# Fused attention and gated convolution: sums' guard planned behind the values, planner costs corrected, pair 0's rows on two queues, last product in two bank pairs, new order tables

## The chip, the cores and the metric

One core of one Trainium2 chip runs the whole kernel in one launch. The metric is device time in microseconds (us) of that core; a run's time is that of one execution, and the median over runs is what counts.

## The reference

```python
# attention: B=8, H=8, S=576, D=64
scores = q @ k.T / sqrt(D)
cum = cumsum(max(s, 0))
bias = -(cum[:, None] - cum[None, :])
scores = where(causal, -1e9, scores + minimum(bias, 0))
scores = scores - scores.max(-1)
attn = exp(scores); attn = attn / (attn.sum(-1) + 1e-9)
x = concat_heads(attn @ v)                 # 8 x 576 x 512
# mixture part: d_ff=1024, kernel 3
h = maximum(x @ w_in, 0)
conv = depthwise_conv3(h, conv_w)          # along the sequence
out = (h * sigmoid(conv)) @ w_out
```

All in float32; products are made of split high and low parts (three matmuls for one).

## The kernel before

The 64 heads go in 32 pairs (`pair(p)`), each head on one half of the 128 partitions. For a pair, TensorE (PE) makes shift scores for row maxima (`sh`, L1103), VectorE (DVE) reduces them (`mx`, L1120 and L1140), PE makes the transposed scores (`sc`, L1227), ScalarE (ACT) exponentiates them into the single tile `pt` (`ex`, L1244), and PE forms the row sums (`sum`, L1330) and then the values (`pv`, L1278), back to back, in one pair of PSUM banks (`pvs`). What follows the sums is a chain: ACT's **guard** (`gd`, L1347) copies them out with a small constant added into `rs`; two DMAs fold them (`fo`, L1353); DVE takes the reciprocal (`inv`, L1360); a DMA stores it (`ri`, L1365) and two spread it (`rb`, L1375). The values are copied out by `vn` (L1384, ACT or DVE), multiplied (`nm`, L1387) and split into `x` (`xh` L1404, `xl` L1408). Four pairs make one batch entry. Its mixture part is `moe_h` (product L1443, relu `re` L1464, convolution centre `ce` L1478 or L1480 and taps L1493, gate `ga` L1507, `mu` L1513, split `uh` L1522 and `ul` L1527), and `moe_o` (product L1591, copies out `oe` L1622 and L1624, stores L1634 and L1637).

PSUM is four pairs of banks (`ps0` to `ps3`), taken by `psb()`. `moe_o` keeps its two output tiles in the two banks of one pair, and the two copies out (`oe`) are separate tasks.

Nothing is ordered by the source. Each step is a task with a cost per engine, dependencies and a tag (its due time plus a shift from the table `DUE`). `Sched.play` runs a list scheduler on these costs, and the instructions of each engine are then emitted in the planned starting order, and every engine works its list strictly in that order. Where the plan leaves PE idle for longer than 0.6 on its clock, filler matmuls on `mask` are put in (`stay_awake`, L1655). Bulk loads (over 200 KB) are limited to two in flight (`FLY`): the third waits for the first.

The guard's dependency in the plan of before, and the first of the two loads for pair 0's rows:

```python
t_grd = add(f"gd{p}", [("ACT", c_act(RS))], [t_sum], tq, guard, alloc=[ri], uses=[pvs])
...
t_e0 = add("dr0", on, [t_cum, *t_pads], -163, d_rows, alloc=[ek], nbytes=42000)
```

Of the kernel before, what the change touches and what calls it, by code (L numbers as in the profile page):

```python
# [35 lines left out]
NDR, NDS = 0, 0  # L36
# [59 lines left out]
    "pads":  # L96
        "0 -413.8 1 1.58 2 -45.35",
    "ind":
# [395 lines left out]
def kernel(  # L494
# [145 lines left out]
    def c_act(n, ptr=0):  # L640
        return 0.19 + n / 1.2e3 + 0.09 * ptr
# [1091 lines left out]
```

## Time and profile before

| what | value |
|---|---|
| runs | 810.8, 808.15, 808.61 us; median 808.61 us |
| profiled execution | 812.8 us, of which the span from first to last instruction is 811.1 us |
| mean granted TensorE clock | 0.977 of full speed |
| busy: PE, PE weight load, DVE, ACT, POOL | 749.0, 629.2, 545.4, 403.8, 289.5 us |
| DMA | 75.48 MB, mean 93 GB/s |

The profiled execution is 4.2 us over the median of the runs. Busy time of an engine counts each instant once in which one of its instructions runs; PE's contains the filler matmuls. In the rows below, `[a <-X]` at the end of a timeline row is the idle time of the engine just before it and what ended that.

### The profile page before, as it was taken

How to read it: one execution, taken by the hardware profiler on the slowest of the kernel's cores; microseconds unless marked ns; L12 is line 12 of the kernel's file. 1: busy time of each engine (PE TensorE's matmuls, PEld its weight loads, DVE VectorE, ACT ScalarE, POOL GpSimd, SP SyncE). 2: the span in 40 equal slices, each digit the busy share in tenths (PEclk: the TensorE clock that was granted, in tenths of full speed). 3: DMA queues.
4: the chain of work that ended last, by engine and by line, in shares of the span. 5: the costliest groups of instructions: out<-in, count | busy, mean ns of one | idle time of the engine just before them, and what ended most of it. 6: DMA issues, size and time to landing. Idle time of an engine off the chain costs nothing. (4 is left out here: it accounts for less than half of the span.)

```text
span 811.1 us, 24282 instructions
## 1 busy us (share of the span) xinstructions
PE 749.0 (92%) x10029; PEld 629.2 (78%) x10029; DVE 545.4 (67%) x1439; ACT 403.8 (50%) x704; POOL 289.5 (36%) x408
## 2 busy tenths in 40 slices
PE   7999999989999899988999898988989988999999
PEld 5776888869787696867887776876868778777987
DVE  7889877666865576886867465574776636756652
ACT  6566554544554455545645364553444434645431
POOL 5534521334136622423133435524316355310000
PEclk9999999999999999999999999989999999999999
DMA  7676413142223422322132233323213322101001
GB/s 224 179 213 213 126 35 120 61 125 62 90 95 99 132 80 86 99 91 90 63 120 64 78 94 103 103 94 94 74 47 105 121 69 86 33 17 43 27 27 40
DMA packets 50088, 75.48 MB, mean 93 GB/s; under 512 B 13690, under 2 KB 26298, under 8 KB 49978
## 3 DMA queue, kind: packets, MB, share of 16 engines
q1 hardware_dynamic: 49978, 73.94, 29.5%
q8 instruction: 78, 1.28, 0.6%
q14 instruction: 32, 0.26, 0.1%
HBM read 63.53 MB, written 10.03 MB: 91 GB/s over the span
## 5 line engine op out<-in xcount | busy, mean ns | idle before, releaser
L1443 PE MATMUL ps<-x,wi 64*128 64x258 f32 (+1 forms) x3072 | 231.2, 301 | 8.9 <-DVE r L1140 3.9
L1443 PEld LDWEIGHTS ps<-x,wi 64*128 64x128 f32 x3072 | 217.8, 190 | 15.7 <-DVE r L1140 4.1
L1591 PE MATMUL ps<-wo,u 64*128 64x512 f32 x1536 | 198.4, 399 | 9.4 <-ACT u L1522 4.2
L1591 PEld LDWEIGHTS ps<-wo,u 64*128 64x128 f32 x1536 | 142.5, 187 | 41.2 <-ACT u L1522 5.5
L1140 DVE CUSTOM_DVE_ANT_0 ps<-ps,rw 128x448 f32<-128x448 f32 (+4 forms) x250 | 109.6, 439 | 68.2 <-POOL rw L1061 41.5
L1244 ACT ACTIVATE pt<-ps,less 128x1024 f32<-128x1024 f32 (+1 forms) x128 | 116.0, 926 | 64.4 <-PE ps L1227 55.1
L1493 DVE SCALAR_TENSOR_TENSOR ct<-ht,cw_sb,ct 128x256 f32<-128x256 f32 (+3 forms) x256 | 124.0, 525 | 11.0 <-POOL rw L1061 6.0
L1227 PE MATMUL ps<-s 64*128 64x288 f32 (+4 forms) x1152 | 114.3, 314 | 14.1 <-ACT pt L1244 4.4
L1061 POOL TENSOR_SCALAR_AFFINE_SELECT rw<-rw 128x256 f32<-128x256 f32 (+1 forms) x125 | 49.0, 397 | 202.5 <-DVE ct L1493 70.4
L1227 PEld LDWEIGHTS ps<-s 64*128 64x128 f32 (+1 forms) x1152 | 86.5, 189 | 22.9 <-ACT pt L1244 7.3
L1278 PE MATMUL ps<-pt,v 128*32 128x448 f32 (+4 forms) x1536 | 92.8, 388 | 0.0
L1255 POOL TENSOR_SCALAR_AFFINE_SELECT pt<-pt 128x256 f32<-128x256 f32 (+1 forms) x115 | 46.1, 421 | 123.8 <-ACT pt L1244 40.9
L1278 PEld LDWEIGHTS ps<-pt,v 128*32 128x32 f32 x1536 | 50.6, 110 | 39.8 <-issue 29.9
L1464 ACT ACTIVATE ht<-ps 128x642 f32<-128x642 f32 (+1 forms) x64 | 41.8, 653 | 73.6 <-PE ps L1443 72.7
L1103 PE MATMUL ps<-s 64*128 64x288 f32 (+4 forms) x384 | 49.2, 312 | 13.0 <-DVE r L1140 8.9
L1513 DVE TENSOR_TENSOR ct<-ct,ht 128x640 f32<-128x640 f32 (+1 forms) x64 | 48.1, 751 | 15.9 <-ACT ct L1507 15.9
L1507 ACT ACTIVATE ct<-ct 128x640 f32<-128x640 f32 (+1 forms) x64 | 43.6, 682 | 26.5 <-DVE ct L1493 26.5
L1347 ACT ACTIVATE rs<-ps 128x144 f32<-128x144 f32 x32 | 9.3, 292 | 90.0 <-PE ps L1278 85.2
L1293 POOL TENSOR_TENSOR ad<-ad,pt 128x640 f32<-128x640 f32 (+2 forms) x45 | 49.9, 1109 | 11.8 <-DVE ct L1493 10.9
L1227 PE MATMUL ps<-eq,ek 64*128 64x288 f32 (+1 forms) x360 | 51.9, 311 | 0.0
L1478 ACT ACTIVATE ct<-ht,cw_sb 128x256 f32<-128x256 f32 (+1 forms) x101 | 49.8, 528 | 2.6
L1103 PEld LDWEIGHTS ps<-s 64*128 64x128 f32 x384 | 32.8, 186 | 22.2 <-DVE r L1140 12.1
(120 smaller groups left out, 943.6 us busy)
## 6 DMA issues: line engine op xcount, KB each, us to landing
raw<-qk SPq DMA_DIRECT2D x32, 576.0 KB
rw<-cum_d SPq DMA_DIRECT2D x25, 576.0 KB
v<-vp SPq DMA_DIRECT2D x32, 320.0 KB
rb<-ri_d SPq DMA_DIRECT2D x64, 144.0 KB
out<-ob SPq DMA_DIRECT2D x32, 256.0 KB
w<-w_in SPq DMA_DIRECT2D x8, 512.0 KB
ht<-w_out SPq DMA_DIRECT2D x8, 256.0 KB
w<-w_out SPq DMA_DIRECT2D x4, 512.0 KB
```

The lines of the kernel that those rows point to most:

```text
L1061: nc.gpsimd.affine_select(out=RW_t[:, :, o : o + k], in_=RW_t[:, :, d : d + k], pattern=[[0, 2], [-1, k]], compare_op=ALU.is_ge, fill=NEG, ...
L1103: nc.tensor.matmul(dst[j], l, m, start=(k == 0), stop=(k == 1 or late))
L1140: nc.vector.tensor_tensor_reduce(out=bank(pb, j, o, o + c1 - c0), in0=bank(pb, j, o, o + c1 - c0), in1=add_, scale=1.0, scalar=acc if c0 e ...
L1227: nc.tensor.matmul(d, l, m, start=(k < 2), stop=(k >= len(steps) - 2 or (t == L and k < 2)), skip_group_check=t == L,)
L1244: nc.scalar.activation(PT[:, :, o : o + w], both(pb, 0, w), AF.Sigmoid, bias=less, scale=0.125,)
L1278: nc.tensor.matmul(bank(pvs, n, o0, o0 + c1 - c0)[gs], vt[0:jt, t, gs], PT_t[g // 2][0:jt, O_T[t] + c0 : O_T[t] + c1], start=(t == 0), sto ...
L1293: tt_on(e)(acc, PT[:, :, P:S] if t == 1 else acc, PT[:, :, O_T[t] : O_T[t] + W_T[t]], op=ALU.add,)
L1443: mm = nc.tensor.matmul(bank(hb, i, 0, XW[hf]), wi[rows[j], k_ // 2, c, f * P : f * P + P], x[rows[j]], start=not turned and k == 0, stop= ...
L1478: nc.scalar.activation(o, src, AF.Copy, scale=w)
L1493: nc.vector.scalar_tensor_tensor(cc[:, lo:hi], h_[:, sh + lo : sh + hi], cw_sb[:, 3 * f + k : 3 * f + k + 1], cc[:, lo:hi], op0=ALU.mult, ...
L1513: nc.vector.tensor_tensor(cc, cc, H_t[ht.slot][:, :, hf : hf + hw], op=ALU.mult)
L1591: mm = nc.tensor.matmul(bank(pb, m, 0, cw_), l, r, start=turned + fp + n == 0, stop=turned == 1 and fp == FP - 1 and n == len(steps) - 1,)
```

## The change

1. `gd` depends on `t_pv` instead of `t_sum`: the planner places the guard behind the values.
2. Costs in the planner: loads of `dr` 1.7 to 1.3 for pair 0 (others had 1.3), `ds` 0.76 to 0.57, `inv` 0.16 to 0.21, `vn` on ACT 0.16 less and on DVE 0.92 to 0.82, `xh` and `xl` 0.07 to 0.1 less.
3. Pair 0's rows: the first head's row load stays on SP's queue (`dr0`), the second's is issued by ACT (`dp0`).
4. `moe_o`'s second copy out depends on the first in the plan, except in the last product; the last product takes two pairs of banks (`pb`, `pb2`), one for each output tile.
5. All shifts in `DUE` are new, so the order on every engine is new.

```diff
 DUE = {
     "x":
-        "s 259.08 clear 322.83 ident 135.65 tab -53.57 hot 112.19 unit 390.52 mrow 347.58 "
...
+        "s 43.07 clear 279.06 ident 94.83 tab -293.61 hot -127.33 unit 452.5 mrow 111.92 "
...
-        def d_rows(e):
-            for j in range(2):
+        def d_rows(e, heads=(0, 1)):
+            for j in heads:
...
-        on = [("SP", 1.7)]
+        on = [("SP", 1.3)]
         if p == 0:
-            t_e0 = add("dr0", on, [t_cum, *t_pads], -163, d_rows, alloc=[ek], nbytes=42000)
+            t_e0 = add("dr0", [("SP", 0.9)], [t_cum, *t_pads], -163, lambda e: d_rows(e, (0,)), alloc=[ek], nbytes=21000)
+            t_e1 = add("dp0", [("ACT", 0.9)], [t_cum, *t_pads], -300, lambda e: d_rows(e, (1,)), uses=[ek], nbytes=21000)
+            sch.follow(t_e0, t_e1)
...
-                   [t_ek, t_nbt] + ([t_e0] if p == 0 else []), (A if late else a_sh) - DRA + 2, level, uses=[ek])
+                   [t_ek, t_nbt] + ([t_e0, t_e1] if p == 0 else []), (A if late else a_sh) - DRA + 2, level, uses=[ek])
...
-        t_shift = add(f"ds{p}", [("ACT", 0.76)] if p < NDS else [("SP", 0.76)], [t_rt, *t_ind], a_sh + 1, d_shift, alloc=[eq],
+        t_shift = add(f"ds{p}", [("ACT", 0.76)] if p < NDS else [("SP", 0.57)], [t_rt, *t_ind], a_sh + 1, d_shift, alloc=[eq],
...
-        t_grd = add(f"gd{p}", [("ACT", c_act(RS))], [t_sum], tq, guard, alloc=[ri], uses=[pvs])
+        t_grd = add(f"gd{p}", [("ACT", c_act(RS))], [t_pv], tq, guard, alloc=[ri], uses=[pvs])
...
-        t_inv = add(f"inv{p}", [("DVE", 0.16)], [t_fold], tq, inverse, uses=[ri])
+        t_inv = add(f"inv{p}", [("DVE", 0.21)], [t_fold], tq, inverse, uses=[ri])
...
         pb, q = psb(), buf("qo")
+        pb2 = psb() if (b, hf) == (B - 1, 1) else pb
...
-                                bank(pb, m, 0, cw_), l, r, start=turned + fp + n == 0,
+                                bank(pb2 if m else pb, m, 0, cw_), l, r, start=turned + fp + n == 0,
...
-                    copy_on(e)(o, bank(pb, m, 0, cw_))
+                    copy_on(e)(o, bank(pb2 if m else pb, m, 0, cw_))
...
-                      [prev], tg, evac, alloc=[ob], uses=[pb, q])
+                      [prev, None if last else t_e], tg, evac, alloc=[ob],
+                      uses=[pb2 if m else pb, q])
```

What stands where. **ACT around the guard of the 22nd pair.** `rs` is the guard, `ct` and `ht` are the convolution's tiles, `ob` an output tile, `vc` the copied values, `pt` the exponentials. Before:

```order
L1464 ACTIVATE ht_101<-ps_67 128x2x321
L1478 ACTIVATE ct_103<-ht_101,cw_sb 128x320 x2
L1464 ACTIVATE ht_102<-ps_65 128x2x257
L1478 ACTIVATE ct_104<-ht_102,cw_sb 128x256 x2
L1347 ACTIVATE rs<-ps_66 128x144
L1522 CAST u_1766<-ct_105 128x512
L1384 COPY vc<-ps_66 128x128
L1384 COPY vc<-ps_66 128x448
```

and in the changed kernel:

```order
L1407 CAST x_90<-rb 128x258
L1467 ACTIVATE ht_101<-ps_67 128x2x321
L1481 ACTIVATE ct_104<-ht_101,cw_sb 128x320
L1510 ACTIVATE ct_103<-ct_103 128x640
L1350 ACTIVATE rs<-ps_64 128x144
L1387 COPY vc<-ps_64 128x128
L1387 COPY vc<-ps_64 128x448
L1247 ACTIVATE pt<-ps_64,less 128x2x288
```

Before, nothing that ACT does is emitted between this pair's first value matmul and its guard, and the cast of `u` stands behind the guard; now a centre and a gate (L1481, L1510) stand in between. Counted over the built programs in the order of emission, from a pair's first value matmul to its guard, ACT had 12 such instructions for all 32 pairs, and has 66, of which 20 are the copies `vc` of the same pair's values. Of the 27 pairs from the sixth on, 5 had an ACT instruction other than `vc` there, and 16 have now.

**DVE around the reciprocal of the 29th pair** (`rc` is the folded sums, L1140 with `ps` the maxima and with `r` alone the read of a maximum). Before:

```order
L1387 TENSOR_TENSOR rb<-vc,rb 128x576
L1384 COPY vc<-ps_67 128x128
L1384 COPY vc<-ps_67 128x448
L1360 RECIPROCAL rc<-rc 128x9
L1140 ISA ps_64,r_94<-ps_64,rw 128x448
L1140 ISA r_94 128x1
L1140 ISA ps_64,r_94<-ps_64,rw 128x448
```

and in the changed kernel:

```order
L1143 ISA ps_64,r_95<-ps_64,rw 128x448
L1143 ISA r_95 128x1
L1143 ISA ps_64,r_95<-ps_64,rw 128x64
L1143 ISA r_95 128x1
L1143 ISA ps_64,r_95<-ps_64,rw 128x64
L1143 ISA r_95 128x1
L1516 TENSOR_TENSOR ct_104<-ct_104,ht_100 128x2x256
L1143 ISA ps_66,r_95<-ps_66,rw 128x320
L1143 ISA r_95 128x1
L1363 RECIPROCAL rc<-rc 128x9
```

The maxima that stood behind the reciprocal stand ahead of it now. Between a pair's first value matmul and its reciprocal DVE had 162 instructions over all pairs, reads not counted, and has 303.

**SP's queue at the start** (`w` is a piece of the weights, `raw` a pair's q and k, `ek` the rows). Before:

```order
L725 DMA pt<-s 64x576
L843 DMA w_10240_119<-w_in 128x4x256
L843 DMA w_10240_121<-w_in 128x4x256
L973 DMA raw_76<-qk 128x1152
L768 DMA grid_d<-pt 64x576
L1010 DMA ek_80<-pt 9x1x576 x2
L1013 DMA ek_80<-pt 2x576
```

and in the changed kernel:

```order
L726 DMA pt<-s 64x576
L844 DMA w_10240_119<-w_in 128x4x256
L974 DMA raw_76<-qk 128x1152
L844 DMA w_10240_121<-w_in 128x4x256
L1011 DMA ek_80<-pt 9x1x576
L1014 DMA ek_80<-pt 2x576
```

Pair 0's q and k go ahead of the second piece of weights, and one of the two row loads is gone from SP (it stands on ACT, ahead of the cast of pair 0's q and k). PE's list has the same 8,572 matmuls of work, and 242 fillers instead of 205: 141 before and 143 now up to the 780th matmul or so, 35 and 70 between there and the end of the last product, 29 in both behind it.

## Rows read from the trace of the kernel before

**Rows 1.** The page's busy times: us, share of the span, instructions.

```profile
PE 749.0 (92%) x10029; PEld 629.2 (78%) x10029; DVE 545.4 (67%) x1439; ACT 403.8 (50%) x704; POOL 289.5 (36%) x408
```

**Rows 2.** Waits over the whole span: us in total, times, longest.

```profile
ACT rs L1347 <- PE ps L1278: 85.2, 30, 6.5
...
DVE ob L1624 <- ACT ob L1624: 42.0, 10, 9.9
...
DVE rc L1360 <- DMA rc<-rs: 36.4, 22, 5.7
...
ACT ct L1507 <- DVE ct L1493: 26.5, 19, 3.6
```

**Rows 3.** Timeline around the guard of the 22nd pair: start, us, instruction.

```profile
499.00 2.87 PE L1278 MATMUL ps<-pt,v 128*32 128x128 f32 x48
499.10 0.82 DVE L1513 TENSOR_TENSOR ct<-ct,ht 128x640 f32<-128x640 f32 x1
...
501.96 0.29 ACT L1347 ACTIVATE rs<-ps 128x144 f32<-128x144 f32 x1 [4.49 <-PE ps L1278]
502.14 0.61 ACT L1522 CAST u<-ct 128x512 fp32r<-128x512 f32 x1
...
502.81 1.94 PE L1591 MATMUL ps<-wo,u 64*128 64x512 f32 x12 [0.94 <-ACT u L1522]
```

**Rows 4.** Timeline around the reciprocal of the 29th pair.

```profile
671.12 0.29 ACT L1347 ACTIVATE rs<-ps 128x144 f32<-128x144 f32 x1 [3.09 <-PE ps L1278]
...
673.87 0.22 DVE L1360 RECIPROCAL rc<-rc 128x9 f32<-128x9 f32 x1 [1.52 <-DMA rc<-rs]
...
676.11 2.25 PE L1443 MATMUL ps<-x,wi 64*128 64x322 f32 x14 [1.88 <-DVE r L1140]
```

**Rows 5.** Windows of 6 us from each of 27 guards: busy us by engine, granted clock.

```profile
111.36:117.36 6.00, 4.58 (x50) 4.08 (x52) 4.98 (x15) 2.84 (x5) 3.40 (x3) 0.88 0.24 60
...
278.40:284.40 6.00, 3.97 (x46) 3.51 (x46) 3.82 (x15) 3.44 (x6) 2.67 (x5) 0.89 0.49 157
...
sum 162.00, PE 129.59 PEld 113.34 DVE 107.31 ACT 98.35 POOL 44.01; mean PE 4.80 PEld 4.20 DVE 3.97 ACT 3.64 POOL 1.63
```

**Rows 6.** Windows of what lies between those, from 100 to 800 us.

```profile
135.05:159.84 24.79, 22.76 (x340) 18.99 (x340) 16.11 (x47) 11.33 (x22) 7.33 (x11) 1.00 0.29 93
...
sum 538.00, PE 518.83 PEld 436.66 DVE 351.10 ACT 243.69 POOL 196.43; mean PE 18.53 PEld 15.59 DVE 12.54 ACT 8.70 POOL 7.02
```

**Rows 7.** The core's span and mean granted clock.

```profile
core 0: 811.1 us, clock 0.977
```

**Rows 8.** Window just behind the guard of the 13th pair; the granted clock is 0.50.

```profile
283.10:286.50 3.40, 2.97 (x22) 2.97 (x24) 2.79 (x12) 0.00 (x0) 1.21 (x4) 0.50 0.31 109
```

**Rows 9.** Timeline: 24 matmuls of one form inside and outside that window.

```profile
283.53 3.38 PE L1443 MATMUL ps<-x,wi 64*128 64x322 f32 x24 [2.00 <-DVE r L1140]
...
492.17 1.95 PE L1443 MATMUL ps<-x,wi 64*128 64x322 f32 x24
```

**Rows 10.** PE's groups by line: the fillers.

```profile
L1655 PE MATMUL ps<-mask 128*128 128x256 bf16 x205 | 28.5, 288 | 3.7 <-POOL mask L677 2.2 <-DVE r L1140 1.1 <-DVE rt L1176 0.4
```

**Rows 11.** Timeline of the start: pair 0's loads, cast and level.

```profile
6.54 0.34 SPq L973 DMA_DIRECT2D raw<-qk  x1
...
7.44 1.71 SPq L1010 DMA_DIRECT2D ek<-pt  x2
...
10.48 1.15 ACT L985 CAST s<-raw 128x1152 fp32r<-128x1152 f32 x1 [1.69 <-DMA raw<-qk]
...
12.06 0.77 ACT L1036 ACTIVATE ek<-ek,nbt 74x576 fp32r<-74x576 f32 x1
```

**Rows 12.** Window of the first 100 us: PE, weight load, DVE, ACT, POOL.

```profile
0.00:100.00 100.00, 90.79 (x1391) 71.71 (x1393) 86.26 (x184) 61.19 (x108) 49.07 (x60) 1.00 0.64 194
```

**Rows 13.** Timeline of the end: the last two copies out.

```profile
806.68 0.59 ACT L1624 COPY ob<-ps 128x512 f32<-128x512 f32 x1 [10.03 <-PE ps L1591]
...
807.30 0.69 DVE L1624 COPY ob<-ps 128x512 f32<-128x512 f32 x1 [9.92 <-ACT ob L1624]
```

More of the change, by code (lines that the diff above doesn't have):

```diff
@@ L91 @@
     "x":
[4 rows of a table removed]
[4 rows of a table added]
     "pads":
-        "0 -413.8 1 1.58 2 -45.35",
+        "0 -12.85 1 -220.76 2 -41.24",
     "ind":
[1 row of a table removed]
[1 row of a table added]
     "cw":
[1 row of a table removed]
[1 row of a table added]
     "wi":
[3 rows of a table removed]
[3 rows of a table added]
     "wo":
[6 rows of a table removed]
[6 rows of a table added]
     "qk":
[9 rows of a table removed]
[9 rows of a table added]
     "hi":
[4 rows of a table removed]
[4 rows of a table added]
     "lo":
[4 rows of a table removed]
[4 rows of a table added]
     "dr":
[4 rows of a table removed]
[6 rows of a table added]
     "dq":
[1 row of a table removed]
[1 row of a table added]
     "eq":
[4 rows of a table removed]
[4 rows of a table added]
     "sh":
[4 rows of a table removed]
[4 rows of a table added]
     "tn":
[4 rows of a table removed]
[4 rows of a table added]
     "sc":
[4 rows of a table removed]
[4 rows of a table added]
     "pv":
[4 rows of a table removed]
[4 rows of a table added]
     "nm":
[4 rows of a table removed]
[4 rows of a table added]
     "fo":
[4 rows of a table removed]
[4 rows of a table added]
     "vn":
[4 rows of a table removed]
[4 rows of a table added]
     "rw":
[3 rows of a table removed]
[3 rows of a table added]
     "rk":
[13 rows of a table removed]
[12 rows of a table added]
 }
@@ L1389, in pair @@
         vc = buf("vc")
-        t_free = add(f"vn{p}", [("ACT", c_act(S) + 0.19), ("DVE", 0.92, False, 3.0)], [t_pv], tq, take,
+        t_free = add(f"vn{p}", [("ACT", c_act(S) + 0.03), ("DVE", 0.82, False, 3.0)], [t_pv], tq, take,
                      alloc=[vc], uses=[pvs])
@@ L1408, in x_lo @@
                 tt_on(e)(xx[:, 1, :], src, xx[:, 0, :].bitcast(F32), op=ALU.subtract)
-        t_xh = add(f"xh{p}", [("ACT", c_act(S) + 0.19), ("DVE", c_cp(S) + 0.15, True, 1.0)], [t_norm], tq,
+        t_xh = add(f"xh{p}", [("ACT", c_act(S) + 0.1), ("DVE", c_cp(S) + 0.08, True, 1.0)], [t_norm], tq,
                    x_hi, alloc=x, uses=[rb])
-        x_done[p] = add(f"xl{p}", [("DVE", c_tt(S) + 0.155, True), ("POOL", c_pool(S) + 0.19, True, 2.0)], [t_xh],
+        x_done[p] = add(f"xl{p}", [("DVE", c_tt(S) + 0.075, True), ("POOL", c_pool(S) + 0.09, True, 2.0)], [t_xh],
                         tq, x_lo, uses=[rb, *x])
@@ L1610, in moe_o @@
                 prev = add(f"o{b}.{hf}.{2 if rest_ else 0}.{turned}{fp}", [("PE", 6 * (cw_ / 2.4e3 + 0.0145))],
-                           deps, tf, o_mm, alloc=[pb, q] if turned + fp == 0 else [],
-                           uses=([us] if rest_ else [u_bufs[b, hf, fp]]) + ([pb] if turned + fp else []),
+                           deps, tf, o_mm, alloc=[pb, q] + ([pb2] if last else []) if turned + fp == 0 else [],
+                           uses=([us] if rest_ else [u_bufs[b, hf, fp]]) + ([pb] + ([pb2] if last else []) if turned + fp else []),
                            mode="r", prev=None if turned and not fp else prev)
         obs = [buf("ob")] if rest_ else [buf("ob"), buf("ob")]
+        t_e = None
         for m in range(1 if rest_ else 2):
```

161 rows, old and new, of the table DUE are left out of this document.

## The prediction

> **What bounds the kernel now.** I began with the busy times. PE has 749.0 of 811.1 us, the other engines at most 545.4 (DVE) and ACT only 403.8 [rows 1]. So PE is the resource, and what can be won in steady state is PE's idle time, PE's time at the lower clock and its fillers; an engine that only holds others up matters through these three.
>
> The list of waits comes next, to see whom the engines wait for. Its longest line is ACT's guard waiting for the value matmuls: 85.2 us in 30 waits, 2.8 each, nearly the 2.87 us that the values take [rows 2, 3]. Two other long lines are of the same kind: DVE's reciprocal waiting for the folded sums, 36.4 us in 22 waits, and DVE's second copy out waiting for ACT's first one, 42.0 us in 10 [rows 2]. These are not costs in themselves, since ACT has time to spare. What counts is what stands behind the waiting instruction on its engine, because each list is worked strictly in order.
>
> The timeline at the 22nd pair shows that. DVE finishes the product that the next cast of `u` needs at 499.10 + 0.82 = 499.92. ACT is free then, but its list has the guard first, and the guard waits until the values end, 4.49 us of ACT's time. The cast starts at 502.14, 2.2 us late, and the output product that wants it leaves PE idle for 0.94 us [rows 3]. At the 29th pair the same lateness runs through DVE: guard at 671.12 after 3.09 us of waiting, reciprocal at 673.87 after 1.52 us of waiting for the fold, the maxima behind it, and then PE, which waits 1.88 us for a maximum to free a pair of banks [rows 4].
>
> Is this the rule or two picked cases? I cut the time from 100 to 740 us into the 6 us from each of the 27 guards in it, and the rest up to 800 us. From the guards on: 162.00 us, PE busy 129.59, so 32.4 idle, 20%. In the rest: 538.00 us, PE busy 518.83, so 19.2 idle, 3.6% [rows 5, 6]. At 3.6% the stretches behind guards would have 5.8 us of idle time. **The excess is 26.6 us.**
>
> The lower clock is the second part. The mean clock is 0.977 [rows 7]; with only the two levels 2.4 and 1.2 GHz, (1 - 0.977)/0.5 x 811.1 = 37.3 us were at the lower one. One such stretch follows the 13th guard: PE had waited 2.00 us for a maximum, then the clock is 0.50 for 3.4 us [rows 8, 9]. In it 24 matmuls take 3.38 us, outside 1.95 [rows 9], so 42% of low-clock time is lost: **15.8 us**. Of the windows at guards that I show, both have a mean clock under 1.00, 0.88 and 0.89 [rows 5]. I count all of the low-clock time to the same cause, though a part of it lies in the rest, where such a stretch runs on. At stake are 26.6 + 15.8 = 42.4 us.
>
> **The change part by part.** *Guard behind the values, and the new order.* The guard's real wait stays: it reads the bank pair that the values are being written to. What changes is what stands ahead of it. Of the 27 later guards 5 had work of ACT other than `vc` planned under the values, now 16 have: 11 of the 22 bare ones are covered, half. At the reciprocal DVE's covering instructions go from 162 to 303. I take **half of 42.4, -21.2 us**. The ends: nothing, if PE's gaps have another cause or move elsewhere; all, -42.4, since the 303 may cover the reciprocal everywhere and that was the way by which PE was hit in [rows 4]. Half is nearer to what the order shows at the guard, the first link.
>
> The Trainium skill (PSUM — Partial Sum Buffer, section "PSUM bank collisions raise a hardware error") says that no two engines may touch one bank and quadrant of partitions at once, also in different columns. By it the guard can never run under the values, as the trace agrees (30 waits ended by the value matmuls), and only the cover counts, which is the sum here; did the change start the guard right after the sums, 2.87 us earlier, all of 42.4 would be in reach.
>
> *Fillers.* 242 instead of 205. 205 take 28.5 us of PE [rows 10], 0.139 each, so 37 more are **+5.1 us**. They stand where the planner itself sees PE idle, so this is idle time that the new order keeps: I count it in full. Lower end 0, where PE would have idled anyhow.
>
> *Second copy out after the first, in the plan.* It removes DVE's waits (42.0 us, of which 9.9 is the idle end [rows 2, 13]), with DVE free for maxima in between. DVE is not the bound, and its effect on PE is in the 42.4 where it lies near a guard; beyond that I take 0, between a gain of some of the 19.2 us of other idle time [rows 6] and nothing.
>
> *Corrected costs.* They change no instruction. Their effect is in the order: counted above.
>
> *Pair 0's rows on two queues, and its q and k ahead.* SP's issue of the two row loads takes 1.71 us [rows 11]; one of them on ACT frees 0.86. ACT idles 1.69 us before the cast of pair 0 [rows 11], which hides the issue; without that cover it would delay cast and level by 0.86. q and k were issued at 6.54, and the cast could start at 10.48; now they go ahead of the second weight piece and no longer hold the cast, so the level (12.06) hangs on its rows. Together **-1.0 us**. Bounds: 0, because DVE is busy 86.26 of the first 100 us and may be what paces them [rows 12], and -1.7.
>
> The Trainium skill (DMA: Bandwidth & Descriptors, section "Issuing engines are not separate DMA queues") says that a second issuing engine saves the issue time only; by that this part gives 0.86 us, and were the transfers separate too it would give the full 1.71.
>
> *Last product in two pairs of banks.* The copies at the end go one after the other, ACT at 806.68, DVE at 807.30 [rows 13]; now DVE needn't wait, 0.62 us less. The two stores are issued one after the other by SP, so I take **-0.4 us** (0 to -0.6). The price is a pair of banks held by the last product, at a time when no pair of heads is left to want one: nothing. If `moe_h` of the last batch still wants them, it waits as long as one product's 24 matmuls, some 2 us.
>
> *Sum.* -21.2 + 5.1 - 1.0 - 0.4 = -17.5 us. Of the profiled execution (812.8; the span is 811.1 and 1.7 lies around it) that leaves 795.3. The median of the runs is 4.2 under that execution, so 808.6 - 17.5 = **791 us**. With the bounds: all recovered and no cost of fillers 808.6 - 42.4 - 1.4 = 765; nothing recovered and fillers in full 808.6 + 5.1 = 814.
>
> **The rivals.** *(a) Nearly everything goes.* For it: 303 against 162 at the reciprocal. Against it: 11 guards still bare, 70 fillers where 35 stood in steady state. All of 42.4, less 5.1, with the 1.4 of start and end: 808.6 - 38.7 = 770.
>
> *(b) The change doesn't do what it says.* The guard has always started at the end of the values; a dependency in the plan moves nothing on the chip, and the gaps belong to the pair's border: `pt` is one tile, so the next pair's exponentials can't start before the values end, and ACT and DVE then get everything at once. For it: idle time of 3.6% elsewhere shows that PE runs well as long as no border is near [rows 6]. Against it: the cast that lay ready for 2.2 us [rows 3]. Nothing recovered, the fillers standing where PE idled before: 808.6 - 1.4 = 807.
>
> *(c) Slower: the guard now stands behind work that waits for DVE.* What was put ahead of it is centre, gate and cast; a gate waits for its taps, 26.5 us in 19 waits, 1.39 each [rows 2]. If the gate ahead of the guard comes that late, the guard, the fold and the reciprocal do too, and the maxima behind that. With all 16 covered guards, 16 x 1.39 = 22.2 us reach PE: 808.6 - 17.5 + 22.2 = 813. It decides from 17.5/1.39 = 13 late guards on. For it: DVE is the second busiest engine and its taps are the last link before a gate. Against it: those waits end after 3.6 us at the longest, and what stands ahead is placed under 2.87 us of values.
>
> **How the numbers follow.** Forecast (half recovered, 780 to 803): 0.56. (a) 0.14, (b) 0.14, (c) 0.16. A change within 0.3%, 2.4 us, is about what a measurement of this kernel can't tell from none. The forecast and (a) are faster, of (b) 0.03 too: 0.73; (b)'s other 0.11 is the same; (c) 0.16 is slower. The range from 770 to 812 takes in forecast and (b), most of (a), and the lower edge of (c); it leaves some 0.06 below and 0.13 above.
>
> **What the profile of the changed kernel would show.** ACT's wait of the guard for the values (85.2 us) falls to 40 or 50, DVE's for the fold (36.4) to under 15, and the second copy's (42.0) to under 20. PE's idle share in the 6 us from each guard falls from 20% to about 12%, and the mean clock rises to about 0.985. If the waits fall and PE's idle share behind guards doesn't, (b) is right. If ACT waits much longer for DVE at the gate and the guard comes later after the values than now (0.1 us), (c) is. A level of pair 0 that starts before 12.06 us shows the start right; a DVE copy at the end that starts with ACT's shows the last part right. The forecast is wrong above all if the new order makes waits of PE that stand in no row here.

## The result and the profile after

The changed kernel takes 765.6 us in the median (763.3 to 768.0), the one before 808.4 on the same chip: ratio 0.947, 95% interval 0.943 to 0.952. The forecast was 791 with a range from 770 to 812, so the direction was right and the time fell out of the range at its lower end. Rival (a), nearly everything goes, gave 770.

The profiled execution took 767.1 us with a span of 765.4, 45.7 less than before. The page's busy times:

```profile
PE 733.4 (96%) x10066; PEld 620.0 (81%) x10066; DVE 543.9 (71%) x1438; ACT 406.2 (53%) x714; POOL 283.0 (37%) x403
```

The core's span and mean granted clock:

```profile
core 0: 765.4 us, clock 0.993
```

PE's share rose from 92% to 96% [rows 1] although it has 37 more matmuls; ACT and DVE do the same work. The mean clock of 0.993 leaves (1 - 0.993)/0.5 x 765.4 = 10.7 us at the lower level, where there were 37.3.

The list of waits over the whole span (us in total, times, longest), the lines that answer to [rows 2] and three more of the chain:

```profile
ACT ct L1510 <- DVE ct L1496: 39.9, 30, 5.3
...
ACT rs L1350 <- PE ps L1281: 24.1, 13, 4.3
...
ACT vc L1387 <- PE ps L1281: 19.1, 7, 5.1
...
DVE ob L1629 <- PE ps L1595: 13.0, 3, 9.7
...
DVE rc L1363 <- DMA rc<-rs: 7.2, 7, 2.4
...
DVE rb L1390 <- DMA rb<-ri_d: 2.7, 6, 0.6
...
ACT ob L1629 <- DVE ob L1629: 1.1, 2, 0.8
```

The guard's wait fell from 85.2 to 24.1 us and is there in 13 pairs instead of 30. A part of it only stands in another line: where the copies `vc` are now ahead of the guard, ACT waits for the values there, 19.1 us that the kernel before didn't have. In all ACT waits 43.2 us for the values, half of what it did. The reciprocal's wait for the fold fell from 36.4 to 7.2; the second copy's wait for the first is gone. The gate's wait for its taps rose from 26.5 to 39.9. What it did to PE is in the windows: the 6 us from each of the 27 guards between 107 and 684 us, and what lies between them from 100 to 755 us, as in [rows 5, 6].

```profile
107.44:113.44 6.00, 6.00 (x76) 5.67 (x78) 5.16 (x20) 3.14 (x7) 2.50 (x4) 1.00 0.28 64
...
155.25:161.25 6.00, 4.84 (x40) 4.19 (x40) 5.29 (x21) 4.43 (x11) 3.11 (x4) 0.58 0.28 99
...
sum 162.00, PE 155.18 PEld 144.63 DVE 121.87 ACT 110.58 POOL 47.23; mean PE 5.75 PEld 5.36 DVE 4.51 ACT 4.10 POOL 1.75
```

```profile
sum 493.00, PE 475.58 PEld 394.13 DVE 332.99 ACT 231.59 POOL 182.42; mean PE 16.98 PEld 14.08 DVE 11.89 ACT 8.27 POOL 6.51
```

Behind the guards PE now idles 6.8 of 162 us, 4.2%, where it was 32.4; in the rest 17.4 of 493, 3.5%, where it was 3.6%. The stretches behind guards have become like any other.

**Where the 45.7 us came from.** PE's idle time fell by 30.1 us (811.1 - 749.0 = 62.1 before, 765.4 - 733.4 = 32.0 now): 25.6 of it behind the guards, 1.8 between them, 2.7 in the first 100 us (9.2 to 6.5). PE's busy time fell by 15.6. The fillers went the other way:

```profile
L1661 PE MATMUL ps<-mask 128*128 128x256 bf16 x242 | 33.1, 284 | 4.5 <-POOL mask L678 2.2 <-ACT ht L1467 1.8 <-DVE r L1143 0.5
```

That is +4.6. The lower clock lasts 26.6 us less, at the prediction's 42% lost time 11.2 us (at 48%, see below, 12.8). Some 7 to 9 us of shorter PE busy time are left without an account; a part of it stands at the output product, whose 1536 matmuls take 193.3 us of PE where they took 198.4.

### The profile page after: what moved, and what is told of

The parts are those of the page before. It is cut to its first block, busy times and chain, and to the rows that moved or that the text cites. A ratio compares the mean times of both kernels' runs of the same rounds, so it can differ in the third digit from the quotient of the medians.

```text
span 765.4 us, 24336 instructions
## 1 busy us (share of the span) xinstructions
PE 733.4 (96%) x10066; PEld 620.0 (81%) x10066; DVE 543.9 (71%) x1438; ACT 406.2 (53%) x714; POOL 283.0 (37%) x403
## 4 chain that ended last, share of the span: by engine, by line
PE 57%; DVE 16%; DMA 12%; POOL 6%; issue 6%; ACT 3%; SPq 1%; POOLq 0%; DVEq 0%; ACTq 0%
PE ps L1595 19%; PE ps L1446 18%; PE ps L1230 9%; PE ps L1281 6%; DVE ps L1143 5%; DMA rw<-cum_d 4%; DVE ct L1496 3%; DMA rb<-ri_d 3%; PE ps L1333 2%; PE ps L1106 2%; POOL ad L1296 2%; DMA raw<-qk 2%; DVE r L1143 1%; POOL rw L1064 1%; POOL pt L1258 1%
## 5 line engine op out<-in xcount | busy, mean ns | idle before, releaser
L1446 PE MATMUL ps<-x,wi 64*128 64x258 f32 (+1 forms) x3072 | 228.5, 297 | 4.0 <-DVE r L1143 2.1
L1446 PEld LDWEIGHTS ps<-x,wi 64*128 64x128 f32 x3072 | 214.2, 187 | 11.0 <-DVE r L1143 2.6
L1595 PE MATMUL ps<-wo,u 64*128 64x512 f32 x1536 | 193.3, 393 | 0.7
L1496 DVE SCALAR_TENSOR_TENSOR ct<-ht,cw_sb,ct 128x320 f32<-128x320 f32 (+3 forms) x256 | 123.6, 524 | 9.7 <-POOL u L1530 4.6
L1230 PE MATMUL ps<-s 64*128 64x288 f32 (+4 forms) x1152 | 109.3, 303 | 7.4 <-ACT pt L1247 3.1
L1230 PEld LDWEIGHTS ps<-s 64*128 64x128 f32 (+1 forms) x1152 | 82.8, 181 | 14.1 <-ACT pt L1247 4.8
L1258 POOL TENSOR_SCALAR_AFFINE_SELECT pt<-pt 128x256 f32<-128x256 f32 (+1 forms) x115 | 43.5, 397 | 108.9 <-DVE ct L1496 41.4
L1510 ACT ACTIVATE ct<-ct 128x640 f32<-128x640 f32 (+1 forms) x64 | 43.7, 683 | 43.3 <-DVE ct L1496 39.9
L1106 PE MATMUL ps<-s 64*128 64x288 f32 (+4 forms) x384 | 50.1, 319 | 9.1 <-DVE r L1143 7.2
L1525 ACT CAST u<-ct 128x512 fp32r<-128x512 f32 x56 | 34.6, 618 | 30.9 <-DVE ct L1516 30.3
L1481 ACT ACTIVATE ct<-ht,cw_sb 128x320 f32<-128x320 f32 (+1 forms) x95 | 47.7, 531 | 2.4
L1143 DVE DVE_READ_ACCUMULATOR2_ANT r<- 128x1 f32 x314 | 44.4, 141 | 0.0
```

The lines of the kernel that those rows point to most:

```text
L1106: nc.tensor.matmul(dst[j], l, m, start=(k == 0), stop=(k == 1 or late))
L1143: nc.vector.tensor_tensor_reduce(out=bank(pb, j, o, o + c1 - c0), in0=bank(pb, j, o, o + c1 - c0), in1=add_, scale=1.0, scalar=acc if c0 e ...
L1230: nc.tensor.matmul(d, l, m, start=(k < 2), stop=(k >= len(steps) - 2 or (t == L and k < 2)), skip_group_check=t == L,)
L1258: nc.gpsimd.affine_select(out=reg, in_=reg, pattern=[[0, 2], [1, dg]], compare_op=ALU.is_ge, fill=0.0, base=0, channel_multiplier=-1,)
L1446: mm = nc.tensor.matmul(bank(hb, i, 0, XW[hf]), wi[rows[j], k_ // 2, c, f * P : f * P + P], x[rows[j]], start=not turned and k == 0, stop= ...
L1481: nc.scalar.activation(o, src, AF.Copy, scale=w)
```

## Experiments

**The theory** at their start was the prediction's mechanism in full strength. The plan of before puts guard, fold and reciprocal some 2.75 us (about the time of the values) before they can run. Every list is worked in order, so the instruction stands at the head of its list, and what PE wants stands behind it. Rivals: that the new order as such, the copies' rule or the corrected costs brought the time; and, later, that any displacement in an order that was searched for costs as much.

Most experiments move instructions in the finished order and leave everything else, by this addition between the planner and the emission (`key` begins as the planned start):

```diff
+    for p in range(NP):
+        key[gd] = (pv.start + 1e-6, -1)
+        key[inv] = (low(inv.start - 2.75, fo), key[inv][1])
...
+    order.sort(key=lambda t: key[t])
```

`low(a, t)` is `a`, or just behind task `t` where that is later. `a_guard_first` has the first of the two lines on `key`, `a_inv_early` the second; `a_chain_early` has the first, and the second's form for `fo`, `inv` and `ri`.

**The changed order with the early places put back.** The guard alone goes right behind its values' place in the order; or the reciprocal alone 2.75 us earlier; or guard, fold, reciprocal and store together.

> The changed kernel with the guard alone moved right behind its pair's values; fold, reciprocal and store stay. Separates ACT's link from SP's and DVE's. If ACT's work stuck behind the guard is the main link: 780 to 795. If the reciprocal on DVE is the main link: 766 to 772, with the guard's wait back at 75 to 90 us and no matter. Rival of the better order: 766 to 772 too, but then the chain moved as a whole gives no more than that.

> The changed kernel with the reciprocal alone moved 2.75 earlier in the order, as far as its fold allows; the guard stays. If DVE's reciprocal is the main link: the wait for the fold at 20 to 40 us and 778 to 795. If ACT's link is: 766 to 772. Rival of the better order: 766 to 772.

> The changed kernel with its own order, and nothing moved but the guard (right behind its pair's values) and fold, reciprocal and store (2.75 earlier in the order), as the old plan believed. Cover theory: the guard's wait is back at 75 to 90 us, the reciprocal's at 25 to 45, PE idle behind guards at 15 to 20%, the clock at 0.98, time 790 to 810. Rival (better order everywhere): time 766 to 775.

Measured: 809.8, 821.8 and 822.2 us beside 808.6 of before; ratios 1.005 [1.001, 1.008], 1.017 [1.011, 1.023], 1.016 [1.010, 1.023]. Against the changed kernel that is +44, +56 and +57 us. All three lie above what the theory had said, 780 to 795, 778 to 795 and 790 to 810. With the guard alone, its wait in the list of waits, and the windows of 6 us behind the guards:

```profile
ACT rs L1350 <- PE ps L1281: 109.5, 30, 8.5
...
DVE rc L1363 <- DMA rc<-rs: 3.6, 3, 1.7
```

```profile
sum 162.00, PE 130.54 PEld 117.37 DVE 118.11 ACT 104.50 POOL 38.58; mean PE 4.83 PEld 4.35 DVE 4.37 ACT 3.87 POOL 1.43
```

With the reciprocal alone, the same two views:

```profile
DVE rc L1363 <- DMA rc<-rs: 58.9, 28, 3.9
...
ACT rs L1350 <- PE ps L1281: 22.2, 12, 4.3
```

```profile
sum 162.00, PE 128.45 PEld 116.72 DVE 93.33 ACT 83.46 POOL 35.37; mean PE 4.76 PEld 4.32 DVE 3.46 ACT 3.09 POOL 1.31
```

PE idles 31.5 and 33.6 us behind the guards, as before the change (32.4). Each link alone, on ACT by the guard or on DVE by the reciprocal, gives back the whole gain, and both together no more than the reciprocal alone. So new table, new costs and new copies don't bring the gain by themselves. In the second case PE waits for DVE's maxima (its list of waits; the three lines are 10.1, 9.0 and 7.5, against 0.4, 7.2 and 0.3 in the changed kernel):

```profile
PE ps L1230 <- DVE r L1143: 10.1, 9, 2.3
PE ps L1106 <- DVE r L1143: 9.0, 8, 2.5
PE ps L1165 <- DVE r L1143: 7.5, 6, 2.2
```

**The order of before with the chain put late.** `b_chain_late` moves guard, fold, reciprocal and store 2.75 us later. `b_all_late` moves the spread, `nm`, `xh` and `xl` with them, `b_all_ob` also the second copies out by 0.62. In these two, 8 pairs' multiplication reads the next pair's copied values; the amount of work is the same. `b_late_clean` is `b_all_late` with those 8 pairs left at their old places. PE's list is that of before in the last three.

```diff
+        key[gd] = (gd.start + 2.75, key[gd][1])
+        for was, t in ((gd, fo), (fo, inv), (inv, ri), (ri, rb), (rb, nm), (nm, xh), (xh, xl)):
+            key[t] = (low(t.start + 2.75, was), key[t][1])
```

> The kernel before with its own order, and nothing moved but the guard, the fold, the reciprocal and the store of each pair, all 2.75 later in the order of emission (work that stood behind them on ACT, SP and DVE now stands ahead). Cover theory (the 26.6 us of PE idle behind guards and the 15.8 us of low clock came from work stuck behind a guard and a reciprocal that stood too early): ACT's wait of the guard for the values falls from 85 to under 45 us, the reciprocal's for the fold from 36 to under 15, PE idle in the 6 us from each guard from 20% to under 10%, time 770 to 788. Rival (the new tables simply give a better order everywhere, and the guard's place is a side matter): waits fall, time stays at 800 to 810.

> The kernel before with PE's list word for word as it was; on the other engines guard, fold, reciprocal, store, spread, product with the values and the split into x are all 2.75 later in the order. The run that moved only guard to store took the guard's and the reciprocal's waits away and won nothing, with PE's idle time moved from behind the guards to elsewhere, and with DVE's product of the values waiting 31.6 us for the spread. Theory now (the lateness was only handed down to the next link, and covering every link of the chain frees PE): product's wait for the spread under 12 us, time 780 to 797. Rival (PE's own order is made for a chain that ends earlier, so its waits for x and for banks stay whatever the others do): 800 to 812.

> As the run before it, and the second copy out of each output product stands 0.62 later, behind the first, as the changed plan has it. Theory: 3 to 8 us less than with the chain alone, DVE's wait of the second copy for the first (35.7 us) under 15. Rival: within 2 us of it, since the copies wait above all for the product.

> The kernel before with PE's list as it was and the chain from guard to split 2.75 later on the other engines in 24 of the 32 pairs; the 8 pairs in which a copied tile would be overwritten before it is used (1 to 4, 11, 12, 28, 30) keep their old places. It repeats the run with all pairs moved, in which those eight read the next pair's copied values, with the whole output right. Theory that PE's own list was made for the early chain: 800 to 808, idle time moved from behind the guards to elsewhere. Theory that covering the links frees PE: 780 to 797.

Measured: `b_chain_late` 809.4, ratio 1.000 [0.997, 1.004]; `b_all_late` 803.7, 0.993 [0.989, 0.996]; `b_all_ob` 805.3, 0.992 [0.989, 0.996]; `b_late_clean` 796.1 beside 806.4, 0.985 [0.980, 0.990]. In `b_chain_late`:

```profile
ACT x L1404 <- DVE rb L1387: 39.7, 16, 4.4
...
DVE rb L1387 <- DMA rb<-ri_d: 31.6, 19, 3.8
...
ACT rs L1347 <- PE ps L1278: 17.9, 10, 5.1
...
DVE rc L1360 <- DMA rc<-rs: 3.8, 5, 0.9
```

and in its windows behind the guards, and then between them up to 800 us:

```profile
sum 162.00, PE 151.24 PEld 138.18 DVE 115.93 ACT 102.02 POOL 60.90; mean PE 5.60 PEld 5.12 DVE 4.29 ACT 3.78 POOL 2.26
...
sum 536.89, PE 499.24 PEld 415.32 DVE 344.83 ACT 244.33 POOL 179.83; mean PE 17.83 PEld 14.83 DVE 12.32 ACT 8.73 POOL 6.42
```

The guard's and the reciprocal's waits are as small as after the change, PE idles only 10.8 us behind the guards, and the time doesn't move: in the rest PE now idles 37.7 us. The theory's range of 770 to 788 failed here, and the rival that these waits are a side matter had the time right, 800 to 810. What speaks against the rival is where the wait went: DVE stands at the multiplication instead, 31.6 us for the spread. Mending two links passed the lateness to the third. With every link late, in 24 of the pairs, 10 us are won, a quarter of the gain. The two rivals for this run were that PE's list, made for a chain that comes early, holds the rest back (800 to 808), and that covering the links frees PE (780 to 797); 796.1 lies at the edge of the second. What holds back the other three quarters isn't shown, and that it is PE's list stays a guess. The wait of the second copy out fell from 36.9 (`b_all_late`) to 18.8 in `b_all_ob` with no time won: the prediction's 0 for it held.

**The planner's inputs one at a time.** `a_nodep` gives the guard its old dependency in the changed kernel; `a_oldtable` has the old shifts, `a_oldcosts` the old costs of `ds`, `inv`, `vn`, `xh` and `xl`, `a_nooe` lets the second copy out go again without the first.

```diff
-        t_grd = add(f"gd{p}", [("ACT", c_act(RS))], [t_pv], tq, ...     (a_nodep)
+        t_grd = add(f"gd{p}", [("ACT", c_act(RS))], [t_sum], tq, ...
-                      [prev, None if last else t_e], tg, evac, ...      (a_nooe)
+                      [prev], tg, evac, ...
```

> The changed kernel with one word undone: the guard depends on the sums again in the plan; all shifts stay, and the planner makes a new order on all engines. If the guard's place carries the gain: the guard's wait at 70 to 110 us and 795 to 820. If not: under 785.

> The changed planner (guard's dependency, costs, copies, start, end) with the shifts of before in the table: a right plan, but shifts that were found for the wrong one. If the planner's rules carry the gain whatever the shifts: 770 to 790. If the shifts that were found with them do: 800 to 825.

> The changed kernel with the corrected costs undone in the plan (ds, inv, vn, xh, xl as before); the shifts stay, the order is another one, the plan's own length is 810.6. If the guard's rule alone makes the plan wrong: 20 to 35 over the plan, a span of 831 to 846. If the costs matter as much: over 50, above 861.

> The changed kernel with one rule undone in the plan: the second copy out doesn't follow the first. The shifts stay, so the whole order is another one, and the plan's own length goes from 737.8 to 771.6. What is asked is how much longer than its plan the span is: 79 for the kernel before (731.7 planned, 811.1 measured), 28 for the changed one (737.8, 765.4), 72 with the guard's rule undone (819.8, 891.5), 18 with the old shifts (829.1, 847.2). If the guard's rule alone makes the plan wrong: 20 to 35 over the plan, a span of 792 to 807. If the copies' rule matters as much: over 50, above 822.

Measured: 888.9, 851.7, 829.0 and 792.2 us; ratios to before 1.097 [1.091, 1.103], 1.050 [1.043, 1.057], 1.025 [1.019, 1.031], 0.980 [0.975, 0.985]. Every one is worse than the changed kernel by 27 to 123 us, but these differences aren't the price of the part: the shifts belong to their planner, and each other planner makes a longer plan out of them. `a_nodep` and `a_oldtable` lie above all that was expected of them (795 to 820, 800 to 825), and their plans are the longest. The planner has a planned length of its own when it ends, which is no time of the chip but can be set beside one. The last column is PE's idle time in the 6 us behind 27 guards, cut for each kernel as above:

| kernel | guard planned behind | planned length | span, us | span over plan | idle behind guards |
|---|---|---|---|---|---|
| before | sums | 731.7 | 811.1 | 79.4 | 32.4 |
| `a_nodep` | sums | 819.8 | 891.5 | 71.7 | 30.4 |
| changed | values | 737.8 | 765.4 | 27.6 | 6.8 |
| `a_oldtable` | values | 829.1 | 847.2 | 18.1 | 12.9 |
| `a_oldcosts` | values | 810.6 | 829.4 | 18.8 | 7.5 |
| `a_nooe` | values | 771.6 | 789.3 | 17.7 | 7.0 |

The windows of `a_nodep`, then of `a_nooe`:

```profile
sum 162.00, PE 131.57 PEld 113.58 DVE 75.11 ACT 97.27 POOL 46.00; mean PE 4.87 PEld 4.21 DVE 2.78 ACT 3.60 POOL 1.70
...
sum 162.00, PE 155.04 PEld 143.84 DVE 106.39 ACT 95.75 POOL 42.81; mean PE 5.74 PEld 5.33 DVE 3.94 ACT 3.55 POOL 1.59
```

With the rule that the chip can't follow, the chip runs 72 to 79 us over the plan; with the right rule 18 to 28, whatever the table, the costs or the copies' rule (20 to 35 was expected of the last two). The idle time behind the guards goes the same way, 30 to 32 us against 7 to 13, though the planner of `a_nodep` differs from that of the changed kernel by the one dependency alone. That is the clearest sign that the rule, and not the new table, took it away. The changed plan is itself 6.1 us longer, and 79.4 - 27.6 - 6.1 = 45.7 is the difference of the spans told in another way, no second proof. The guard's dependency in the otherwise unchanged kernel, and the new table in the unchanged planner, were not tried on the chip: with either the planner gets stuck, with no bank pair left that could come free.

**The fillers at the end.** `a_notail` stops the fillers early (on the planner's clock), which takes 32 away.

```diff
-GAP, TILL = 0.6, 740.0
+GAP, TILL = 0.6, 700.0
```

> The changed kernel without the 29 fillers behind the last product and the 3 ahead of its end; all other lists stay. In both traces the span ends 1.1 us after the last of those fillers. If they set the end: 1 to 2 us less than the changed kernel, 763.5 to 765. If the last stores do: the same within 0.5 us.

Measured: 764.0, ratio 0.946 [0.941, 0.951], not told apart from the changed kernel. The last product ends at 757.67 and the span at 762.0, 4.3 later; in the changed kernel it is 760.96 and 765.4. The fillers behind the last product don't set the end.

**Early against late.** The experiments so far had moved the chain of the changed order in one direction only. Three more moved the reciprocal alone, 2.75 us later, 1.375 us later and 1.375 us earlier. In all three the lists of PE, ACT and POOL are those of the changed kernel row by row.

```diff
+        key[inv] = (inv.start + 2.75, key[inv][1])     (a_inv_late; 1.375 in a_inv_late1)
+        for was, t in ((inv, ri), (ri, rb)):           (store and spread stay behind it)
+            key[t] = (low(t.start, was), key[t][1])
```

> The changed kernel with the reciprocal alone 2.75 us later in the order on DVE (its store and spread behind it where they would precede it); the lists of PE, ACT and POOL are the same row by row. If being early is what costs, being late costs little: the plan leaves 6.3 us or more between a reciprocal and the multiplication that wants its result, so the fold wait falls from 7.2 to about 0, the wait of the multiplication for the spread rises from 2.7 to 20 or 30, and the time is 766 to 780 us. If any displacement from the searched order costs what the early one did, the time is 805 to 820.

> The changed kernel with the reciprocal alone 1.375 us later; the lists of PE, ACT and POOL are the same. If being early is what costs, 764 to 770 us, with the wait of the multiplication for the spread under 15. If any displacement costs, about as much as the step of the same size in the other direction, 785 or more.

> The changed kernel with the reciprocal alone 1.375 us earlier, half of the earlier step; the lists of PE, ACT, POOL and SP are the same. If DVE's standing still is the price, it goes with the wait: with 2.75 the fold wait rose by 51.7 us and the time by 56, so here the wait should be 25 to 35 us and the time 785 to 800. If a displaced order costs as such, the time is near that of the full step, 810 to 822.

Measured: 805.2, 781.1 and 777.4 us; ratios to before 0.998 [0.995, 1.001], 0.969 [0.963, 0.975], 0.962 [0.958, 0.966]. **The theory that only being early costs fell here**: it had 766 to 780 for `a_inv_late`, and the rival that any displacement costs as much had 805 to 820, which 805.2 just meets. The half steps fit neither: 781.1 lies between 764 to 770 and 785 or more, and 777.4 under both 785 to 800 and 810 to 822. In `a_inv_late` DVE's reciprocal hardly waits any more, and the multiplication does, for the spread:

```profile
DVE rb L1390 <- DMA rb<-ri_d: 36.8, 18, 4.9
...
DVE rc L1363 <- DMA rc<-rs: 1.7, 1, 1.7
```

Set side by side, with DVE's two waits on the chain added up:

| reciprocal's place | time, us | over changed | wait for fold + for spread, us |
|---|---|---|---|
| 2.75 earlier | 821.8 | +56.2 | 58.9 + 1.4 = 60.3 |
| 1.375 earlier | 777.4 | +11.8 | 25.1 + 4.5 = 29.6 |
| as in the changed kernel | 765.6 | 0 | 7.2 + 2.7 = 9.9 |
| 1.375 later | 781.1 | +15.5 | 3.5 + 16.9 = 20.4 |
| 2.75 later | 805.2 | +39.6 | 1.7 + 36.8 = 38.5 |

The time has its lowest point where both waits together are shortest, and it rises on either side, though not in proportion to them (+11.8 us with 29.6 us of waits, +15.5 with 20.4). Too early, DVE stands at the reciprocal; too late, it stands at the next link, whose place is now early for its own input. The full step costs more than twice the half one in both directions. One mechanism fits all five, a reading made after the runs: an instruction heads its list before its input is there. How much of the rise is owed to the standing still and how much to the lateness of `x` itself isn't told apart. For the standing still speak PE's waits in `a_inv_late`, which grow at the read maxima of DVE (from 7.2 and 2.1 us in the changed kernel) and name `x` nowhere:

```profile
PE ps L1106 <- DVE r L1143: 11.5, 10, 2.8
...
PE ps L1446 <- DVE r L1143: 7.9, 3, 4.5
```

For the lateness speaks that ACT's cast of `x` waits longer for the multiplication too, 50.4 us instead of 38.5.

## Why the prediction was right in direction and wrong in size

**What bounds the kernel: right.** The idle time behind the guards and the low clock were the place of the gain. I put 26.6 + 15.8 = 42.4 us at stake. That the runs' medians differ by 42.8 is luck: 36.8 of the 42.4 came, and the rest came from elsewhere.

**Half of 42.4: this step failed.** I counted the pairs in which ACT got some other work under the values, 16 of 27 and so 11 of 22 bare ones, and took that as the share that goes, -21.2 us. Recovered were 25.6 of the 26.6 us, and 26.6 of the 37.3 us at the low clock, which is 11.2 of the 15.8: 36.8 us. With that term alone put right the sum gives 776 us. The count is low as well: in the order of both plans, from a pair's values to its guard, I find 9 of the 27 with such work before and 21 now, so 12 of 18 bare ones; two thirds would have given 784. But cover was the wrong measure altogether. ACT does still wait half as long for the values as it did (43.2 of 85.2 us), and yet PE's idle time behind the guards is nearly gone: 4.2% is hardly over the 3.5% elsewhere. As I read it, a bare guard still waits, but the plan knows how long, and little that PE wants soon is planned behind it. I had allowed for that at the reciprocal ("the 303 may cover the reciprocal everywhere") and gave it a chance of 0.14. The experiments show that neither link may be out of place: either one early gave back all of it.

**The rest up to 766** are terms that I put at nothing or too low: 1.8 us of idle time between the guards, 2.7 instead of 1.0 at the start, and the 7 to 9 us of PE's busy time, of which the prediction has no word.

**The 42% are a little low.** The 24 matmuls of [rows 9] end at 286.91, and from 286.53 on the granted clock is 1.00 again. Without these 0.38 us on both sides, 1.57 us of work take 3.00, and 48% are lost.

**Fillers: the size right.** +5.1 said, +4.6 of PE's busy time measured. That they cost the kernel as much isn't shown: the one run with fewer fillers takes away those at the end, where they cost nothing.

**Start: nearly right.** -1.0 said; the level starts 1.4 us sooner (timeline of the start, the two row loads now by ACT and SP):

```profile
6.52 1.33 ACTq L1011 DMA_DIRECT2D ek<-pt  x1
6.53 0.93 SPq L1011 DMA_DIRECT2D ek<-pt  x1
8.12 1.14 ACT L986 CAST s<-raw 128x1152 fp32r<-128x1152 f32 x1
...
10.63 0.76 ACT L1039 ACTIVATE ek<-ek,nbt 74x576 fp32r<-74x576 f32 x1
```

The cast starts at 8.12 instead of 10.48 [rows 11], so the weights no longer hold it up. That the level's 1.4 us reach the end wasn't tested by itself; PE's idle time in the first 100 us fell by 2.7. SP's issue of the rows takes 0.93 us where the two took 1.71, so 0.78 is saved there, near the 0.86 said.

**End: the mechanism right, the time not.** DVE's copy starts with ACT's, as said (timeline of the end):

```profile
760.96 3.34 PE L1661 MATMUL ps<-mask 128*128 128x256 bf16 x29
761.06 0.58 ACT L1629 COPY ob<-ps 128x512 f32<-128x512 f32 x1 [10.40 <-PE ps L1595]
761.10 0.69 DVE L1629 COPY ob<-ps 128x512 f32<-128x512 f32 x1 [9.71 <-PE ps L1595]
761.67 0.81 SPq L1643 DMA_DIRECT2D out<-ob  x2
```

From the last product to the end of the span it takes 765.4 - 760.96 = 4.4 us, where it took 4.5. The -0.4 was 0.1: SP issues both stores behind the copies, and the copy that got 0.62 us earlier doesn't bring the end forward.

**Rivals.** (a) was nearest, 770 against 766. (b), the change doesn't do what it says, fell with the windows. For (c), slower by gates that come late, the sign that I named is there: the gate's waits rose by 13.4 us and 11 times, and 14 of the 32 guards now start more than 0.5 us after their values, one of them 3.45, where before all started within 0.15. The price of 16 x 1.39 isn't to be seen in PE's idle time, so that sign doesn't tell a slower kernel from a faster one. Several of these guards only stand behind the copies of the same values.

**What stays open.** The 7 to 9 us of PE's busy time. Why the changed kernel is 27.6 over its plan and the three longer plans only 18: it may be that a shorter plan has less slack, and no run tests it. Whether the rise with the reciprocal's place is peculiar to the chain of the sums: no instruction outside it was moved alone, so the rival that any move out of a searched order costs as much is not excluded.

## What to carry to other kernels

Where a planner's order feeds in-order lists, each dependency in the plan must be one that the chip can keep: here a copy planned beside matmuls into its own banks started behind them all 32 times (0.09 to 0.15 us after the last), and 32 such instructions at a place 2.75 us off cost 40 to 56 us (the reciprocal in both directions). In this case all of the excess idle time at that border was the better size for such a change, not how many of the waits get covered. Set the measured span beside the planned length: a large difference that lies at one kind of task points to a wrong rule. Moving the first links by hand only passed the wait to the third; mend the rule and plan anew.

## What was not expected of the hardware

The low clock now comes in two stretches only, and each comes with a wait of PE for a read maximum just before, 2.70 us up to 156.41 and 1.99 us up to 315.10. Windows around the first:

```profile
151.00:153.00 2.00, 2.00 (x44) 1.83 (x36) 2.00 (x1) 0.00 (x0) 1.96 (x1) 1.00 0.00 0
153.71:157.00 3.29, 0.59 (x5) 0.55 (x6) 2.93 (x9) 3.13 (x9) 1.58 (x2) 0.87 0.83 270
157.00:160.00 3.00, 3.00 (x30) 2.85 (x28) 2.41 (x11) 1.94 (x4) 1.53 (x3) 0.50 0.08 12
160.00:163.00 3.00, 3.00 (x30) 2.35 (x26) 2.32 (x9) 1.40 (x2) 0.41 (x1) 0.50 0.28 80
```

PE is busy throughout from 157 on and still has 0.50 of full speed, 1.2 GHz, up to some 163 us; so this wait of 2.7 us cost PE more than its 2.7 us, and the list of waits shows none of that part. Not every such wait has this behind it: in the kernel before PE waited 2.43 us up to 174.68, and the granted clock of the next 5.3 us is 1.00.
